# Longer loads for four heads and a shorter load of W2's last rows in a two-layer decode kernel

## The chip, the cores and the metric

The kernel runs on one core of one Trainium2 chip. The metric is the device time of one execution in microseconds; the time given for a kernel is the median of several runs, here 1349.29 us over 3 runs (1348.77 to 1350.27).

## The reference

One token of width 640 goes twice through attention and an MLP, with the same weights and the same cache in both layers:

```python
def _A_ref(x, k_cache, v_cache, wq, wo):
    q = (x @ wq) as 32 heads of 128
    scores = q . k_cache * DH ** -0.5      # 32 heads x 8192 keys x 128
    p = softmax(scores)
    return (p . v_cache) @ wo
def _B_ref(x, w1, w2):
    return maximum(x @ w1, 0) @ w2         # 640 -> 1728 -> 640
x = x + _A_ref(layernorm(x), ...)          # layer 0
x = x + _B_ref(layernorm(x), w1, w2)
x = x + _A_ref(layernorm(x), ...)          # layer 1, the same cache again
x = x + _B_ref(layernorm(x), w1, w2)
```

All of it is float32. The cache of one head is 4 MiB of keys and 4 MiB of values, so one pass over the 32 heads reads 256 MiB. The cache is larger than the on-chip memory and has to be read once for each layer, save what stays on the chip between the two.

## The kernel before

**Order of the work.** Layer 0 goes through heads 0 to 31, layer 1 through heads 31 to 0. What layer 0 read last stays on the chip and is what layer 1 needs first: the last piece of head 29's keys, the last three units of head 30 and all of head 31 are kept (KEPT, 3960 places of 32 bytes in each of 128 partitions). Each head is worked in the same steps: `scores` (L499, TensorE, four matmuls for each piece of keys), `row_maxima` and `exponentials` (VectorE and ScalarE), `values` (L554, TensorE, four matmuls for each piece of values), `output`. At the end of a layer stands the MLP, which reads W2 in 12 blocks that pass through the same ring as the cache, and two more blocks that stay on the chip in `w2_t`.

**The ring and its loads.** Keys, values and W2's twelve blocks go through one tile, `ring`, of RING = 4760 places in each partition. `UNITS` (L42 to 64) says into which units and pieces a head is cut. The list `todo` is the order of all loads; it is written out ahead (L149 to 167), and `pump` (L207) takes its first entry whenever there is room: for an entry without a place, `place` (L181) looks for the tightest gap that holds it whole, for the others `is_free` asks whether the slots are free. Room comes from `release` (L239), which is called behind the last matmul that reads a piece. So each load stands in SyncE's queue behind the one ahead of it, and waits there until the pieces that lay in its place were read. All loads of the ring are issued at L221. One load is one DMA: 128 rows, one for each partition, of as many bytes as the load has places times 32.

**Heads 2 to 26** are loaded by `turning` as whole heads, or in two or three parts where the ring ends; a head is one block in DRAM, with 64 KB for each partition, and a part reads a piece of each of these 64 KB. **Heads 27 to 31** are loaded by units (`all_of`, L127): in DRAM each of their units is a block of its own, the rows of its 128 partitions one behind the other. In layer 0 these heads pass through the first 3072 places alone (L189), since the rest is for what is kept and for W2; four units have a place of their own (`apart`, L123). Layer 1's loads of heads 29, 28 and 27 start where W2's blocks and then the kept pieces have been read. Head 30's two units that are not kept are read into `wct` and `mix` (`load_beside`, L227).

**W2's remainder.** The 1728 rows of W2 are 12 blocks of 128 and 192 rows more. These 192 are laid into two blocks: 128 rows, and 64 rows with 64 rows of zeros behind them (L1043 to 1046). Both are loaded with one DMA of 640 KB on ScalarE's queue at head 7 of layer 0 (L799), and `times_rows` uses only the first 64 partitions of the second block (`rows = 2 * half`).

**ScalarE's queue** also carries the loads of Wq and Wo (L269 to 278), W1 and the row of Wo that is mixed with W1 (L797, L802). `due` (L783) issues those that belong to a head when the head is opened.

Of the kernel before, what the change touches and what calls it, by code (L numbers as in the profile page):

```python
# [15 lines left out]
P = 128  # L16
D = 640
H = 32
# [22 lines left out]
FULL = range(2, 27)  # L41
UNITS = {h: [("kv", K_ALL + V_ALL)] if h <= FULL[-1] else WHOLE for h in range(H)}  # L42
UNITS[0] = [("kv", K_ALL + V_ALL[:3] + [(3, 0, 2), (3, 2, 2)])]
PARTS = {(0, 0): [4, 9], (1, 26): [4, 8], (1, 25): [4, 8], (1, 2): [4, 8], (1, 1): [2, 4, 6, 8], (1, 0): [2, 4, 6, 7, 8, 9]}
UNITS[28] = HALVES
# [17 lines left out]
UNITS[31] = HALVES[:2] + LAST  # L63
DROPPED = {29: 9, 30: 2}
KEPT = 3960
W2_PLACES = 800
# [6 lines left out]
SLOT = RUN // 2  # L73
# [21 lines left out]
F_TILES = 3  # L95
H_CUT = 2 * P
F_REST = 2
FB = 4 * F_TILES + F_REST
W2_RUNS = [range(0, 4), range(4, 8), range(8, 10), range(10, 12)]
UNITS["w2"] = [("w", list(run)) for run in W2_RUNS]  # L100
W2_ALL = [("w2", i) for i in range(len(W2_RUNS))]
RING = KEPT + W2_PLACES


@with_exitstack
def decode_kernel(ctx: ExitStack, tc: tile.TileContext, x, kv, wqo, w1, w2, w2_rest, out):
    nc = tc.nc
# [14 lines left out]
    assert sum(size(UNITS[h][i]) for h, i in kept) == KEPT  # L122
    apart = {(29, 9): (3800, KEPT), (30, 0): (4464, 4544), (30, 1): (4544, RING), (30, 2): (3072, 3800)}  # L123
    beside = [(1, u) for u in order[::-1] if u[0] == 30 and u not in kept]
    todo = []

    def all_of(layer, u):  # L127
        todo.append((layer, u, 0, len(UNITS[u[0]][u[1]][1]), None))

# [7 lines left out]
    def turning(layer, heads, slot):  # L137

        for h in heads:
            for a, end in parts_of(layer, h):  # L140
                while a < end:
                    b = min(end, a + SLOTS - slot)
                    todo.append((layer, (h, 0), a, b, SLOT * slot))
                    slot = (slot + b - a) % SLOTS
                    a = b

    def anywhere(layer, h):
        for a, b in parts_of(layer, h):
            todo.append((layer, (h, 0), a, b, None))  # L149

    for h in range(FULL[0]):
        anywhere(0, h)
    turning(0, FULL, 16)
    for h in range(FULL[-1] + 1, H):
        for i in range(len(UNITS[h])):
            all_of(0, (h, i))
    for u in W2_ALL:
        all_of(0, u)
    for h in range(H)[:FULL[-1]:-1]:
        if h != 30:  # L160
            for i in range(len(UNITS[h])):
                if (h, i) not in kept:
                    all_of(1, (h, i))
    anywhere(1, FULL[-1])
# [4 lines left out]
    for u in W2_ALL:  # L169
        all_of(1, u)  # L170
    source = {}
    for us, dram in ((order, kv), (W2_ALL, w2)):
        o = 0
        for u in us:
            n = 8 * P * size(UNITS[u[0]][u[1]])
            source[u] = dram[o : o + n].rearrange("(p m) -> p m", p=P)
            o += n
    live = {}
# [28 lines left out]
    def pump():  # L207
        while todo:
            layer, u, first, last, at = todo[0]
            unit = UNITS[u[0]][u[1]]  # L210
            ns = [wide(kind_of(unit, t), piece) for t, piece in enumerate(unit[1])]
            n = sum(ns[first:last])
            if at is None:
                at = place(layer, u, n)
                if at is None:
                    return
            elif not is_free(at, n):
                return
            todo.pop(0)
            o = 8 * sum(ns[:first])  # L220
            nc.sync.dma_start(ring[:, 8 * at : 8 * (at + n)], source[u][:, o : o + 8 * n])  # L221
            for t in range(first, last):
                live[layer, u, t] = at, ns[t]
                at_of[layer, u, t] = ring, 8 * at
                at += ns[t]

    def load_beside(where, at, n):  # L227
        layer, u = beside.pop()
        kind, pieces = UNITS[u[0]][u[1]]
        assert 8 * size(UNITS[u[0]][u[1]]) == n  # L230
        nc.sync.dma_start(where[:, at : at + n], source[u])
        for t, piece in enumerate(pieces):
            at_of[layer, u, t] = where, at
            at += 8 * wide(kind, piece)
# [464 lines left out]
    def attention_and_mlp(L, xr, s):  # L699
# [83 lines left out]
        def due(h):  # L783
# [14 lines left out]
            if L == 0 and where == 7:  # L798
                nc.scalar.dma_start(w2_t, w2_rest)  # L799
            if where == 8:  # L800
# [250 lines left out]
def _laid_out(A_x, A_k_cache, A_v_cache, A_wq, A_wo, B_w1, B_w2):  # L1051
# [4 lines left out]
    o = 0  # L1056
    for h in range(H):
        for unit in UNITS[h]:
            n = 8 * size(unit)
            block = kv[o : o + P * n].reshape(P, n)  # L1060
            o += P * n
            a = 0
            for t, piece in enumerate(unit[1]):
                if kind_of(unit, t) == "k":
                    r, c, m = piece
                    part = k[h, :, :, r, c : c + m]
                else:
                    b, r, m = piece
                    part = v[h, :, :, r : r + m, b]
                part = part.reshape(P, -1)  # L1070
                block[:, a : a + part.shape[1]] = part
                a += part.shape[1]
# [7 lines left out]
    for g in range(NG):  # L1080
# [7 lines left out]
        "w2": w2,  # L1088
        "w2_rest": rows[:, 4 * F_TILES :],
    }  # L1090
# [24 lines left out]
```

## Time and profile before

| what | value |
|---|---|
| median of 3 runs | 1349.29 us |
| the profiled execution, its own time | 1349.0 us |
| its span from the first instruction to the last | 1347.2 us |
| TensorE busy | 797.8 us (59%) |
| VectorE busy | 248.3 us (18%) |
| ScalarE busy | 58.5 us (4%) |
| moved by DMA | 574.52 MB, 426 GB/s over the span |

How to read the rows: times are microseconds from the start of the span unless a column says ns. PE is TensorE, DVE VectorE, ACT ScalarE, SP SyncE; a "q" behind a name means its sequencer, where DMAs are issued and waits are spent. L221 is line 221 of the kernel. A row of DMA issues gives the size of one load and the median time from its issue until it has landed. DMA share is the mean busy share of the 16 DMA engines.

### The profile page before, as it was taken

The numbers are of one execution on the slowest core, as the hardware profiler recorded it, in microseconds if no ns is written. First come the engines' busy times: TensorE is split into PE (matmuls) and PEld (weight loads), VectorE is DVE, ScalarE is ACT, GpSimd is POOL, SyncE is SP. The second block draws the span as 40 slices with busy tenths as digits, with TensorE's granted clock in tenths as the row PEclk, the third lists the DMA queues.
The fourth block names the chain that finished last, engine by engine and source line by source line (L and its number), as shares of the span: only waits on it lengthen the run. The fifth ranks groups of instructions, "written<-read, shape, count | busy, mean of one in ns | idle before, by whom it ended". The sixth has DMA issues, their size and how long they took to land.

```text
span 1347.2 us, 13344 instructions
## 1 busy us (share of the span) xinstructions
PE 797.8 (59%) x5966; PEld 261.2 (19%) x5966; DVE 248.3 (18%) x774; ACT 58.5 (4%) x149; POOL 2.9 (0%) x10
## 2 busy tenths in 40 slices
PE   3564445563655664667688754455466654656667
PEld 1121111111211211112252211112121111211214
DVE  1121111121212121112122211122111121111212
ACT  0000000000000000000000000000000000000000
POOL 0000000000000000000000000000000000000000
PEclk9688777778977886788798777898778788878889
DMA  9999999999999999999999999999999999999997
GB/s 413 429 427 437 430 439 428 438 420 428 442 434 422 441 427 423 446 419 419 425 385 425 435 432 436 424 441 429 437 430 430 424 437 436 434 419 438 424 426 326
DMA packets 22673, 574.52 MB, mean 426 GB/s; under 512 B 2516, under 2 KB 2648, under 8 KB 5464
## 3 DMA queue, kind: packets, MB, share of 16 engines
q1 hardware_dynamic: 19592, 529.84, 91.6%
q10 hardware_dynamic: 3024, 43.83, 7.7%
q8 instruction: 47, 0.77, 0.2%
q14 instruction: 10, 0.08, 0.0%
HBM read 573.65 MB, written 0.00 MB: 426 GB/s over the span
## 4 chain that ended last, share of the span: by engine, by line
DMA 65%; PE 26%; DVE 5%; ACT 1%; issue 1%; another core or an unknown queue 1%; ACTq 0%; SPq 0%; DVEq 0%
DMA ring<-in_kv 65%; PE ps L499 13%; PE outs L554 7%; DVE h_t L510 2%; ACT p L524 1%; DVE pt L528 1%; PE pm L515 1%; PE acc L468 1%; PE px L424 1%; DVE p L591 1%; PE px L456 0%; PE px L675 0%; DMA ring<-in_w 0%; DVE pT L530 0%
## 5 line engine op out<-in xcount | busy, mean ns | idle before, releaser
L499 PE MATMUL ps<-ring,spread_q 128*32 128x512 f32 (+3 forms) x2104 | 324.3, 765 | 312.2 <-DMA ring<-in_kv 307.3
L554 PE MATMUL outs<-ring,pT 128*4 128x512 f32 (+1 forms) x2032 | 258.9, 648 | 48.4 <-DVE pT L530 24.4
L499 PEld LDWEIGHTS ps<-ring,spread_q 128*32 128x32 f32 x2104 | 78.2, 137 | 493.2 <-issue 338.5
L510 DVE TENSOR_REDUCE h_t<-ps 128x1 f32<-128x512 f32 x64 | 44.3, 692 | 611.1 <-PE ps L499 611.1
L524 ACT ACTIVATE p<-ps,h_t 128x512 f32<-128x512 f32 x64 | 44.0, 687 | 1223.2 <-DVE h_t L522 1223.2
L554 PEld LDWEIGHTS outs<-ring,pT 128*4 128x4 f32 x2032 | 51.3, 91 | 211.0 <-issue 172.8
L601 PE MATMUL pm<-ones,p 128*128 128x1 f32 x120 | 22.9, 260 | 95.0 <-DVE p L591 95.0
L587 DVE TENSOR_SCALAR p<-outs,ind 128x128 f32<-128x128 f32 x60 | 21.1, 351 | 269.0 <-PE outs L554 269.0
L591 DVE SCALAR_TENSOR_TENSOR p<-outs,ind,p 128x128 f32<-128x128 f32 x180 | 63.1, 351 | 6.4
L528 DVE STREAM_TRANSPOSE pt<-p 128x512 f32<-128x512 f32 x64 | 46.5, 727 | 58.4 <-ACT p L524 58.4
L515 PE MATMUL pm<-row_of,h_t 128*128 128x16 f32 x128 | 26.3, 281 | 49.6 <-DVE h_t L510 48.9
L601 PEld LDWEIGHTS pm<-ones,p 128*128 128x128 f32 x120 | 17.8, 188 | 151.5 <-DVE p L591 150.2
L515 PEld LDWEIGHTS pm<-row_of,h_t 128*128 128x128 f32 x128 | 20.0, 196 | 109.8 <-DVE h_t L510 108.0
L675 PE MATMUL px<-w_t,wct 128*128 128x448 f32 (+1 forms) x80 | 36.7, 574 | 1.0 <-ACT wct L668 1.0
L424 PE MATMUL px<-pair,ln_xc 128*32 128x256 f32 x280 | 34.6, 396 | 4.4 <-ACT mix L683 4.4
L468 PE MATMUL acc<-pair,o_cols 128*32 128x320 f32 x224 | 36.2, 469 | 0.0
L424 PEld LDWEIGHTS px<-pair,ln_xc 128*32 128x32 f32 x280 | 15.7, 113 | 21.4 <-ACT mix L683 8.5
L522 DVE TENSOR_REDUCE h_t<-pm 128x1 f32<-128x16 f32 x64 | 11.2, 175 | 33.0 <-PE pm L515 33.0
L468 PEld LDWEIGHTS acc<-pair,o_cols 128*32 128x32 f32 x224 | 12.9, 117 | 16.8 <-issue 15.7
L675 PEld LDWEIGHTS px<-w_t,wct 128*128 128x128 f32 x80 | 13.8, 197 | 10.8 <-issue 9.3
L530 DVE COPY pT<-pt 128x64 f32<-128x64 f32 x64 | 14.4, 224 | 2.2
L605 DVE COPY o_cols<-pm 128x1 f32<-128x1 f32 x56 | 8.9, 159 | 28.4 <-PE pm L601 28.4
(130 smaller groups left out, 212.1 us busy)
## 6 DMA issues: line engine op xcount, KB each, us to landing
ring<-in_kv SPq DMA_DIRECT2D x24, 4096.0 KB, 31.1
ring<-in_kv SPq DMA_DIRECT2D x11, 6144.0 KB, 36.1
ring<-in_kv SPq DMA_DIRECT2D x31, 2048.0 KB, 35.1
pair<-in_wqo ACTq DMA_DIRECT2D x13, 2560.0 KB, 25.8
ring<-in_kv SPq DMA_DIRECT2D x14, 1024.0 KB, 15.1
ring<-in_w SPq DMA_DIRECT2D x4, 1280.0 KB, 25.9
w_t<-in_w ACTq DMA_DIRECT2D x1, 4320.0 KB, 27.5
pair<-in_wqo ACTq DMA_DIRECT2D x3, 1280.0 KB, 13.1
```

The source lines that it names most:

```text
L424: nc.tensor.matmul(pq[32 * j : 32 * j + 32, :n], xc[:, c : c + 1].to_broadcast([P, 32]), wq_t[g][:, c, j * n : (j + 1) * n], start=(c == 0 ...
L468: nc.tensor.matmul(acc[32 * half : 32 * half + 32, : 2 * DR], col.to_broadcast([P, 32]), wt[:, 2 * half * DR : 2 * (half + 1) * DR], start ...
L499: nc.tensor.matmul(hd.ps[32 * g : 32 * g + 32, c : c + n], spread_q[:, 3 - r : 35 - r], tile_of[:, at + g * n : at + (g + 1) * n], start=f ...
L510: nc.vector.tensor_reduce(hd.nm, hd.ps, AX.X, ALU.max, negate=True)
L515: nc.tensor.matmul(pt[:, :16], hd.nm.to_broadcast([P, P]), row_of.rearrange("p g r -> p (g r)"), start=True, stop=True,)
L524: nc.scalar.activation(hd.p, hd.ps, AF.Exp, bias=hd.low, scale=1.0, accum_out=hd.l)
L528: nc.vector.transpose(pt, hd.p)
L554: nc.tensor.matmul(hd.out[32 * g : 32 * g + 4, r : r + m].rearrange("p r d -> p (r d)"), hd.pT[:, 4 * i : 4 * i + 4], tile_of[:, v : v + m ...
L587: nc.vector.tensor_scalar(oc[:, 0], hd.out[:, 0], ind[:, :1], 0.0, op0=ALU.mult, op1=ALU.add)
L591: nc.vector.scalar_tensor_tensor(oc[:, r], hd.out[:, r], ind[:, r : r + 1], oc[:, r - 1], op0=ALU.mult, op1=ALU.add,)
L601: nc.tensor.matmul(pt[:, :1], oc[:, 3], ones, start=True, stop=True)
L675: nc.tensor.matmul(pt[:, :n], wct[:, c], w1_t[:, c, f : f + n], start=(c == 0), stop=(c == NB - 1),)
```

## The change

**Loads.** `todo` entries now hold a list of pieces that may come from several units, so one load can carry several units that lie one behind the other in DRAM. For that, the rows of DRAM are made longer: all units of a head (for heads 29 and 30: all units of both, in the order that `ROWS` gives) stand in one row for each partition. A row is 64 KB for heads 0 to 28 and 31, and 128 KB for the joint block of 29 and 30. The order of heads stays; within head 29 the last of its keys that are not kept (unit 6) move ahead of its values.

| loads (KB each) | before | after |
|---|---|---|
| layer 0, head 27 | 4096, 4096 | 8192 |
| layer 0, head 28 | 2048 x4 | 4096, 4096 |
| layer 0, head 29 | 1024, 1024, 512, 640, 1024, 1024, 256, 1024, 1024, 640 | 3456, 640, 4096 |
| layer 0, head 30 | 320, 864, 2912, 2048, 2048 | 1184, 2912, 2048, 2048 |
| layer 0, head 31 | 2048, 2048, 2048, 1024, 512, 512 | the same |
| layer 1, head 29 | 1024, 1024, 512, 640, 1024, 1024, 256, 1024, 1024 | 1024, 1024, 512, 640, 3328, 1024 |
| layer 1, head 28 | 2048 x4 | 4096, 2048, 2048 |
| layer 1, head 27 | 4096, 4096 | the same |
| layer 1, head 1 | 2048 x4 | 4096, 4096 |

That is 11 loads fewer in layer 0 and 6 fewer in layer 1.

**W2's remainder.** The 640 KB load becomes one of 320 KB (the 128 rows), and the 64 rows come in eight loads of eight rows of 2560 bytes, one at each of heads 16 to 23 of layer 0, on ScalarE's queue. The eight rows of one load go to partitions that lie four apart: 0, 4, ... 28, then 1, 5, ... 29, and so on to 35, 39, ... 63. The rows of zeros are neither stored nor loaded.

```diff
--- before.py
+++ after.py
@@ -41,7 +41,7 @@
 FULL = range(2, 27)
 UNITS = {h: [("kv", K_ALL + V_ALL)] if h <= FULL[-1] else WHOLE for h in range(H)}
 UNITS[0] = [("kv", K_ALL + V_ALL[:3] + [(3, 0, 2), (3, 2, 2)])]
-PARTS = {(0, 0): [4, 9], (1, 26): [4, 8], (1, 25): [4, 8], (1, 2): [4, 8], (1, 1): [2, 4, 6, 8], (1, 0): [2, 4, 6, 7, 8, 9]}
+PARTS = {(0, 0): [4, 9], (1, 26): [4, 8], (1, 25): [4, 8], (1, 2): [4, 8], (1, 1): [4, 8], (1, 0): [2, 4, 6, 7, 8, 9]}
 UNITS[28] = HALVES
 UNITS[29] = [
     ("k", K_ALL[:1]),
@@ -62,6 +62,34 @@
 ] + HALVES[2:]
 UNITS[31] = HALVES[:2] + LAST
 DROPPED = {29: 9, 30: 2}
+ROWS = [[(h, i) for i in range(len(UNITS[h]))] for h in range(29)]
+ROWS.append([(29, i) for i in (0, 1, 2, 3, 6, 4, 5, 7, 8)] + [(30, 2), (29, 9), (30, 0), (30, 1), (30, 3), (30, 4)])
+ROWS.append([(31, i) for i in range(len(UNITS[31]))])
+ENDS = [
+    [(27, 0), (27, 1)],
+    [(28, 0), (28, 1)],
+    [(28, 2), (28, 3)],
+    ROWS[29][:5],
+    [(29, 9)],
+    ROWS[29][5:9],
+    [(30, 0), (30, 1)],
+    [(30, 2)],
+    [(30, 3)],
+    [(30, 4)],
+] + [[u] for u in ROWS[30]]
+STARTS = [
+    [(29, 0)],
+    [(29, 1)],
+    [(29, 2)],
+    [(29, 3)],
+    ROWS[29][4:8],
+    [(29, 8)],
+    [(28, 0), (28, 1)],
+    [(28, 2)],
+    [(28, 3)],
+    [(27, 0)],
+    [(27, 1)],
+]
 KEPT = 3960
 W2_PLACES = 800
 WIDE = 64
@@ -96,6 +124,7 @@
 H_CUT = 2 * P
 F_REST = 2
 FB = 4 * F_TILES + F_REST
+LAST_AT = [32 * half + i for half in range(2) for i in range(4)]
 W2_RUNS = [range(0, 4), range(4, 8), range(8, 10), range(10, 12)]
 UNITS["w2"] = [("w", list(run)) for run in W2_RUNS]
 W2_ALL = [("w2", i) for i in range(len(W2_RUNS))]
@@ -103,7 +132,7 @@
 
 
 @with_exitstack
-def decode_kernel(ctx: ExitStack, tc: tile.TileContext, x, kv, wqo, w1, w2, w2_rest, out):
+def decode_kernel(ctx: ExitStack, tc: tile.TileContext, x, kv, wqo, w1, w2, w2_rest, w2_last, out):
     nc = tc.nc
     consts = ctx.enter_context(tc.tile_pool(name="consts", bufs=1))
     work = ctx.enter_context(tc.tile_pool(name="work", bufs=1))
@@ -120,12 +149,12 @@
     order = [(h, i) for h in range(H) for i in range(len(UNITS[h]))]
     kept = [u for u in order if u[0] >= min(DROPPED) and u[1] >= DROPPED.get(u[0], 0)]
     assert sum(size(UNITS[h][i]) for h, i in kept) == KEPT
-    apart = {(29, 9): (3800, KEPT), (30, 0): (4464, 4544), (30, 1): (4544, RING), (30, 2): (3072, 3800)}
+    apart = {(29, 9): (3800, KEPT), (30, 0): (4464, RING), (30, 2): (3072, 3800)}
     beside = [(1, u) for u in order[::-1] if u[0] == 30 and u not in kept]
     todo = []
 
-    def all_of(layer, u):
-        todo.append((layer, u, 0, len(UNITS[u[0]][u[1]][1]), None))
+    def all_of(layer, us):
+        todo.append((layer, [(u, t) for u in us for t in range(len(UNITS[u[0]][u[1]][1]))], None))
 
     def parts_of(layer, h):
 
@@ -140,41 +169,43 @@
             for a, end in parts_of(layer, h):
                 while a < end:
                     b = min(end, a + SLOTS - slot)
-                    todo.append((layer, (h, 0), a, b, SLOT * slot))
+                    todo.append((layer, [((h, 0), t) for t in range(a, b)], SLOT * slot))
                     slot = (slot + b - a) % SLOTS
                     a = b
 
     def anywhere(layer, h):
         for a, b in parts_of(layer, h):
-            todo.append((layer, (h, 0), a, b, None))
+            todo.append((layer, [((h, 0), t) for t in range(a, b)], None))
 
     for h in range(FULL[0]):
         anywhere(0, h)
     turning(0, FULL, 16)
-    for h in range(FULL[-1] + 1, H):
-        for i in range(len(UNITS[h])):
-            all_of(0, (h, i))
-    for u in W2_ALL:
-        all_of(0, u)
-    for h in range(H)[:FULL[-1]:-1]:
-        if h != 30:
-            for i in range(len(UNITS[h])):
-                if (h, i) not in kept:
-                    all_of(1, (h, i))
+    for us in ENDS + [[u] for u in W2_ALL]:
+        all_of(0, us)
+    for us in STARTS:
+        all_of(1, us)
     anywhere(1, FULL[-1])
     turning(1, FULL[-2:-1], 0)
     turning(1, FULL[:-2][::-1], 8)
     for h in range(FULL[0])[::-1]:
         anywhere(1, h)
     for u in W2_ALL:
-        all_of(1, u)
+        all_of(1, [u])
     source = {}
-    for us, dram in ((order, kv), (W2_ALL, w2)):
-        o = 0
-        for u in us:
-            n = 8 * P * size(UNITS[u[0]][u[1]])
-            source[u] = dram[o : o + n].rearrange("(p m) -> p m", p=P)
-            o += n
+    o = 0
+    for row in ROWS:
+        n = 8 * sum(size(UNITS[h][i]) for h, i in row)
+        block = kv[o : o + P * n].rearrange("(p m) -> p m", p=P)
+        o += P * n
+        a = 0
+        for h, i in row:
+            source[h, i] = block, a
+            a += 8 * size(UNITS[h][i])
+    o = 0
+    for u in W2_ALL:
+        n = 8 * P * size(UNITS[u[0]][u[1]])
+        source[u] = w2[o : o + n].rearrange("(p m) -> p m", p=P), 0
+        o += n
     live = {}
     at_of = {}
 
@@ -206,29 +237,35 @@
 
     def pump():
         while todo:
-            layer, u, first, last, at = todo[0]
-            unit = UNITS[u[0]][u[1]]
-            ns = [wide(kind_of(unit, t), piece) for t, piece in enumerate(unit[1])]
-            n = sum(ns[first:last])
+            layer, pieces, at = todo[0]
+            ns = []
+            for u, t in pieces:
+                unit = UNITS[u[0]][u[1]]
+                ns.append(wide(kind_of(unit, t), unit[1][t]))
+            n = sum(ns)
             if at is None:
-                at = place(layer, u, n)
+                at = place(layer, pieces[0][0], n)
                 if at is None:
                     return
             elif not is_free(at, n):
                 return
             todo.pop(0)
-            o = 8 * sum(ns[:first])
-            nc.sync.dma_start(ring[:, 8 * at : 8 * (at + n)], source[u][:, o : o + 8 * n])
-            for t in range(first, last):
-                live[layer, u, t] = at, ns[t]
+            u, t = pieces[0]
+            block, o = source[u]
+            unit = UNITS[u[0]][u[1]]
+            o += 8 * sum(wide(kind_of(unit, i), unit[1][i]) for i in range(t))
+            nc.sync.dma_start(ring[:, 8 * at : 8 * (at + n)], block[:, o : o + 8 * n])
+            for (u, t), m in zip(pieces, ns):
+                live[layer, u, t] = at, m
                 at_of[layer, u, t] = ring, 8 * at
-                at += ns[t]
+                at += m
 
     def load_beside(where, at, n):
         layer, u = beside.pop()
         kind, pieces = UNITS[u[0]][u[1]]
         assert 8 * size(UNITS[u[0]][u[1]]) == n
-        nc.sync.dma_start(where[:, at : at + n], source[u])
+        block, o = source[u]
+        nc.sync.dma_start(where[:, at : at + n], block[:, o : o + n])
         for t, piece in enumerate(pieces):
             at_of[layer, u, t] = where, at
             at += 8 * wide(kind, piece)
@@ -796,7 +833,10 @@
             if L == 0 and where == 4:
                 nc.scalar.dma_start(w1_t, w1)
             if L == 0 and where == 7:
-                nc.scalar.dma_start(w2_t, w2_rest)
+                nc.scalar.dma_start(w2_t[:, 0], w2_rest)
+            if L == 0 and 16 <= where < 24:
+                a = LAST_AT[where - 16]
+                nc.scalar.dma_start(w2_t[a : a + 32 : 4, 1], w2_last[where - 16])
             if where == 8:
                 of, nth = divmod(last, HG)
                 nc.scalar.dma_start(
@@ -1054,12 +1094,13 @@
     v = v.transpose(0, 1, 5, 4, 2, 3, 6).reshape(H, P, 4, 4, NBL, DH)
     kv = np.empty(H * P * SK * 2, k.dtype)
     o = 0
-    for h in range(H):
-        for unit in UNITS[h]:
-            n = 8 * size(unit)
-            block = kv[o : o + P * n].reshape(P, n)
-            o += P * n
-            a = 0
+    for row in ROWS:
+        n = 8 * sum(size(UNITS[h][i]) for h, i in row)
+        block = kv[o : o + P * n].reshape(P, n)
+        o += P * n
+        a = 0
+        for h, i in row:
+            unit = UNITS[h][i]
             for t, piece in enumerate(unit[1]):
                 if kind_of(unit, t) == "k":
                     r, c, m = piece
@@ -1086,7 +1127,8 @@
         "wqo": wqo,
         "w1": np.asarray(B_w1).reshape(NB, P, DFF).transpose(1, 0, 2),
         "w2": w2,
-        "w2_rest": rows[:, 4 * F_TILES :],
+        "w2_rest": rows[:, 4 * F_TILES],
+        "w2_last": np.stack([rows[a : a + 32 : 4, 4 * F_TILES + 1] for a in LAST_AT]),
     }
```

## Rows read from the trace of the kernel before

**Rows 1.** The page: its span, and the rate of all DMA in 40 slices.
```profile
span 1347.2 us, 13344 instructions
...
GB/s 413 429 427 437 430 439 428 438 420 428 442 434 422 441 427 423 446 419 419 425 385 425 435 432 436 424 441 429 437 430 430 424 437 436 434 419 438 424 426 326
```

**Rows 2.** The page, the chain that ended last, shares by engine.
```profile
DMA 65%; PE 26%; DVE 5%; ACT 1%; issue 1%; another core or an unknown queue 1%; ACTq 0%; SPq 0%; DVEq 0%
```

**Rows 3.** Stretches: length, busy PE, PEld, DVE, ACT, POOL, PEclk, DMA share, GB/s.
```profile
20.00:560.00 540.00, 297.33 (x1994) 89.05 (x1986) 93.36 (x276) 21.65 (x55) 0.00 (x0) 0.79 1.00 432
600.00:640.00 40.00, 29.36 (x220) 8.65 (x216) 10.13 (x33) 1.56 (x4) 0.00 (x0) 0.89 0.99 418
640.00:690.00 50.00, 33.81 (x364) 14.06 (x360) 9.32 (x29) 3.08 (x8) 0.00 (x0) 0.85 1.01 424
690.00:700.00 10.00, 9.17 (x188) 6.55 (x176) 2.83 (x15) 0.37 (x3) 0.00 (x0) 1.00 0.80 318
700.00:716.00 16.00, 13.33 (x184) 6.56 (x184) 3.86 (x17) 0.78 (x2) 1.10 (x2) 1.00 1.01 406
760.00:1300.00 540.00, 313.91 (x2102) 95.34 (x2102) 97.35 (x290) 22.83 (x58) 0.00 (x0) 0.81 1.00 431
```

**Rows 4.** Waits of SyncE's queue from 588 to 760 us: total, times, longest.
```profile
SPq L221 <- DMA ring<-in_kv: 46.7, 17, 9.4
```

**Rows 5.** Three single loads: time of issue, then size and time to landing.
```profile
569.52 0.33 SPq L221 DMA_DIRECT2D ring<-in_kv  x1
...
ring<-in_kv SPq DMA_DIRECT2D x1, 4096.0 KB, 29.6
...
576.76 0.33 SPq L221 DMA_DIRECT2D ring<-in_kv  x1
...
ring<-in_kv SPq DMA_DIRECT2D x1, 4096.0 KB, 32.1
...
636.49 0.33 SPq L221 DMA_DIRECT2D ring<-in_kv  x1
...
ring<-in_kv SPq DMA_DIRECT2D x1, 640.0 KB, 15.1
```

**Rows 6.** Head 27's scores on TensorE, in order of time: start, length.
```profile
605.10 1.06 PE L499 MATMUL ps<-ring,spread_q 128*32 128x512 f32 x8
...
606.62 2.78 PE L499 MATMUL ps<-ring,spread_q 128*32 128x512 f32 x24
```

**Rows 7.** The second load of head 28's keys: issue, size and time to landing.
```profile
592.01 0.33 SPq L221 DMA_DIRECT2D ring<-in_kv  x1
...
ring<-in_kv SPq DMA_DIRECT2D x1, 2048.0 KB, 26.6
```

**Rows 8.** W2's last load in layer 0: issue, size and time to landing.
```profile
696.55 0.33 SPq L221 DMA_DIRECT2D ring<-in_w  x1
...
ring<-in_w SPq DMA_DIRECT2D x1, 640.0 KB, 4.9
```

**Rows 9.** Head 31's scores in layer 1 (chain); the fourth load of head 29.
```profile
707.43 3.71 PE ps L499 x32
...
702.30 0.33 SPq L221 DMA_DIRECT2D ring<-in_kv  x1
...
ring<-in_kv SPq DMA_DIRECT2D x1, 640.0 KB, 13.6
```

**Rows 10.** W2's remainder on ScalarE's queue; ScalarE's waits from 340 to 520 us.
```profile
166.52 0.34 ACTq L799 DMA_DIRECT2D w_t<-in_w_rest  x1
...
w_t<-in_w_rest ACTq DMA_DIRECT2D x1, 640.0 KB, 24.7
...
ACT p L524 <- DVE h_t L522: 178.7, 9, 30.1
```

**Rows 11.** The page's DMA issues: loads of three quarters of a head.
```profile
ring<-in_kv SPq DMA_DIRECT2D x11, 6144.0 KB, 36.1
```

## The prediction, made before the change was run

> **What bounds the kernel now.** I read the page first. Its rate of DMA stands between 385 and 446 GB/s in all slices but the last, over a span of 1347.2 us [rows 1], and the chain that ended last is DMA for 65% [rows 2]. A chain alone doesn't say whether the transfers or the latency between them are the limit, so I cut the run into stretches next [rows 3]. From 20 to 560 us, where heads of 8192 KB come in one to three loads, the 16 DMA engines are busy with a share of 1.00 and move 432 GB/s; from 760 to 1300 us it is 1.00 and 431. The kernel there is as long as its bytes. Three stretches around the change of layer move less: 418 GB/s (600 to 640 us), 424 (640 to 690) and 406 (700 to 716), all at a share of 0.99 to 1.01, so the engines are not out of work there but do their work in smaller portions. One stretch is short of work: 690 to 700 us, with a share of 0.80 and 318 GB/s, where layer 0's MLP has to be finished before places come free.
>
> Last I looked at SyncE's queue between 588 and 760 us: 17 times, 46.7 us in all, a load there waited for the landing of an earlier load and not for a reader [rows 4]. The change lessens such waits, as it has fewer loads. They are priced at nothing: the DMA engines had a share of 1.00 while they lasted [rows 3], so what they held back would have stood in line anyway.
>
> **The price of one load.** In layer 0 the second half of head 27 lands at 576.76 + 32.1 = 608.86 us, and the last unit of head 29 at 636.49 + 15.1 = 651.59 us [rows 5]. In these 42.73 us come the 14 loads of heads 28 and 29, 16384 KB, and 1280 KB of Wo, together 18.09 MB. At 432 GB/s that is 41.87 us; 0.86 us is left, 0.06 us for each of the 14 loads. The long loads next to them check the rate: head 27's two halves land 608.86 - 599.12 = 9.74 us apart, 4.19 MB at 431 GB/s [rows 5].
>
> Seventeen loads fewer then give 17 x 0.06 = 1.0 us. All of it lies on the path, because the DMA engines are the bound on either side. The bounds: nothing, if the shortfall of these stretches comes from something other than the number of loads; and all of it, if longer loads restore 432 GB/s, which is (14/432) x 40 + (8/432) x 50 + (26/432) x 16 = 1.3 + 0.9 + 1.0 = 3.2 us [rows 3]. I take 1.0, worked out from the loads themselves; the stretch from 700 us keeps its four short first loads, and layer 0's head 31 keeps its six.
>
> **What longer loads hold back.** A longer load waits for a longer gap, and its readers wait for all of it. There are three places.
>
> Head 27 of layer 0 is now one load. It goes where the second half went (576.76 us) and lands at 608.8 us with it, whereas TensorE was ready for its keys at 605.10 us and took until 609.40 [rows 6]. So the keys are read by 608.8 + 4.3 = 613.1 us. Behind that stands the load of head 28's values, for which head 27's keys must have gone. The queue meanwhile holds head 28's keys, which land as before at 592.01 + 26.6 = 618.6 us [rows 7]. How early must a load be issued to follow without a gap? W2's last load met a nearly idle queue and took 4.9 us to land [rows 8]; 1.5 us of that are its 655 KB at 432 GB/s, so 3.4 us are lead. The values have to go by 618.6 - 3.4 = 615.2 us; they go at 613.1, which leaves 2.1 us. Price: nothing; if that cover is gone, each us that TensorE is later costs one.
>
> In layer 1, units 6, 4, 5 and 7 of head 29 become one load that needs both halves of head 31's keys read: 707.43 + 3.71 = 711.1 us [rows 9]. The load ahead of it lands at 702.30 + 13.6 = 715.9 us, less 3.4 of lead is 712.5 us: 1.4 us of cover, price nothing, bound 1.0 us. Behind this load in SyncE's queue stand all others of layer 1; the next ones (unit 8, head 28's keys) need head 30's keys and head 31's values read, which comes later still, so none of them is held up by it. Head 28's keys as one load land with their second half. Head 1's two loads of 4096 KB need gaps of 1024 places in place of 512; head 2's 8192 KB stand in line ahead of them, price nothing.
>
> Head 29's unit 6 now lands ahead of its values, and its values land together. In layer 0 its values are read after their last piece is there, and then head 30's 1184 and 2912 KB stand in line, 9.7 us at 432 GB/s. Nothing is charged.
>
> **W2's remainder.** The zeros are 64 x 2560 bytes = 0.164 MB, 0.38 us at 432 GB/s. That is the gain if all 16 engines share it. The bounds follow from who is relieved: if eight engines had carried the zeros, each has 20,480 bytes less, 0.76 us at 432/16 = 27 GB/s, which counts in full if the slowest engine is among them and not at all if it isn't.
>
> The eight new loads cost between nothing and 8 x 0.06 = 0.48 us; I take half, as each has only eight rows: 0.24 us. Net -0.14 us. ScalarE issues each in 0.34 us [rows 10] just ahead of a head's exponentials. It waited 178.7 us for VectorE in nine waits between 340 and 520 us [rows 10], so the issues are hidden; if not, it is 8 x 0.34 = 2.7 us. They go at heads 16 to 23 of 32, and the one load of 640 KB took 24.7 us beside long loads [rows 10], so TensorE doesn't wait for them in the MLP.
>
> [...]
>
> **The sum.** -1.02 (loads) - 0.38 + 0.24 (W2) + 0 (holding back) = -1.2 us against the profiled execution's 1349.0, that is 1347.8. The median of the runs shown is 0.3 us higher, 1349.29; on that scale the forecast is 1348.1 us. A change within 0.2% (2.7 us) can't be told from none in this kernel, so I forecast no change that shows.
>
> **Rivals.**
> 1. *The short loads were the whole shortfall.* Then 3.2 us come back and W2's relief is the full 0.76: 1349.29 - 4.0 = 1345.3 us. For it: the share is 1.0 at 418 GB/s, so the engines lose time within the transfers [rows 3]. Against it: 0.06 us for a load explains all the excess between 609 and 652 us. Chance 0.16.
> 2. *Slower: the row spacing of 128 KB.* Heads 29 and 30 now lie in DRAM with 128 KB from one partition's row to the next; head 28's and 27's rows are 64 KB apart. The joint block is read for 16384 KB in layer 0, 7552 KB in layer 1 and 1184 KB beside the ring: 25.7 MB, 59.5 us at 432 GB/s. If that spacing cost x%, the time would rise by 0.595 us for each percent: 5% gives 1349.29 - 1.2 + 3.0 = 1351.1 us, and it shows as slower from 6.6% on (3.9 us), 1352.0. Half the rate would be 59.5 us, 1407.6. Against it: the eleven loads of 6144 KB and the other parts of heads already read pieces of rows 64 KB apart [rows 11], in stretches that run at 432 GB/s [rows 3]. No row shows 128 KB. Chance of 6.6% or more: 0.05.
>    [...]
> 3. *The cover at head 27 is gone.* TensorE reads head 27's keys over 6 us later than worked out; the DMA engines then stand idle for 4 us and more and the result is slower, some 1352 us. It would take other work of TensorE between the landing and the scores; rows 6 show 4.3 us for all of it, the side work included. Chance 0.03.
>
> **How the numbers follow.** The forecast has 0.76; its own range runs from -1.02 - 0.76 to 0.48 + 1.0, that is 1347.5 to 1350.8 us. The range given reaches down into rival 1, to 1345.6, and ends at 1350.8 us. Faster by over 0.2% is rival 1: 0.16. Slower by over 0.2% is rivals 2 and 3: 0.08. The rest, 0.76, is no change.
>
> **What would show it.** Right: the stretches 600 to 640 and 640 to 690 us some 3 to 5 GB/s faster, 690 to 700 us as poor as it is, head 27's scores some 4 us later, and the stretch around 613 to 620 us at a share near 1. The rival of the spacing would show as heads 29 and 30 moving at well under 420 GB/s in both layers. Wrong: a drop of the DMA share around 615 or 713 us, ScalarE waiting in its queue at heads 16 to 23, or a gain that lies outside 560 to 760 us, which no step here provides.

## The result, and the profile after

The changed kernel takes 1354.56 us (median of 6 runs, 1353.61 to 1355.95) against 1349.40 us before (6 runs): 5.2 us slower, ratio 1.0037 with a 95% interval of 1.0027 to 1.0047. Forecast were 1348.1 us and no change that shows.

The two profiled executions have spans of 1347.2 and 1353.4 us, 6.2 us apart. The page of the changed kernel, the lines that answer to [rows 1]:

```profile
span 1353.4 us, 13316 instructions
...
GB/s 417 421 432 432 445 418 435 435 425 440 429 428 425 438 431 431 440 423 385 424 377 409 434 430 428 433 439 429 441 434 425 427 437 431 432 425 435 426 427 300
```

One slice stands out whose counterpart before kept up with its neighbours (419 GB/s): the nineteenth, 609 to 643 us, at 385 GB/s. The stretches of the changed kernel (some lie within others), columns as in [rows 3]:

```profile
20.00:560.00 540.00, 298.19 (x1994) 89.13 (x1986) 93.26 (x276) 21.65 (x55) 0.00 (x0) 0.79 1.00 432
600.00:620.00 20.00, 12.04 (x68) 3.55 (x64) 3.69 (x12) 0.78 (x2) 0.00 (x0) 0.74 0.84 348
612.00:614.00 2.00, 2.00 (x16) 0.55 (x12) 0.00 (x0) 0.00 (x0) 0.00 (x0) 0.50 0.68 295
614.00:616.00 2.00, 2.00 (x12) 0.20 (x4) 0.00 (x0) 0.00 (x0) 0.00 (x0) 0.50 0.51 205
612.00:620.00 8.00, 5.41 (x32) 1.45 (x28) 1.96 (x6) 0.78 (x2) 0.00 (x0) 0.71 0.69 260
712.00:718.00 6.00, 5.08 (x32) 1.01 (x24) 0.77 (x2) 0.00 (x0) 0.00 (x0) 0.73 0.83 348
760.00:1300.00 540.00, 325.19 (x2086) 96.98 (x2082) 97.97 (x291) 22.93 (x58) 0.00 (x0) 0.79 1.00 431
```

and two of the same stretches before:

```profile
612.00:620.00 8.00, 5.70 (x50) 1.71 (x51) 2.56 (x10) 0.00 (x0) 0.00 (x0) 1.00 1.00 424
712.00:718.00 6.00, 6.00 (x70) 2.04 (x74) 1.82 (x4) 0.78 (x2) 0.00 (x0) 1.00 1.01 421
```

The long stretches are untouched, 432 and 431 GB/s in both. The DMA engines run short of work in two places where they had none missing: at 612 to 620 us (share 0.69 for 1.00, 8 x 0.31 = 2.5 us of their time) and at 712 to 718 us (0.83 for 1.01, 1.1 us). And the granted clock of TensorE (third column from the end) is lower in both, 0.71 and 0.73 for 1.00.

**At head 27 of layer 0.** TensorE's instructions in order (start, length), then the issue of head 28's values on SyncE:

```profile
604.19 0.38 PE L638 MATMUL pm<-ones,p 128*128 128x1 f32 x2 [1.65 <-DVE p L628]
608.30 1.94 PE L536 MATMUL ps<-ring,spread_q 128*32 128x512 f32 x8 [3.72 <-DMA ring<-in_kv]
610.16 1.01 PE L476 MATMUL px<-sel,q_row 64*128 64x2 f32 x4
611.11 5.31 PE L536 MATMUL ps<-ring,spread_q 128*32 128x512 f32 x24
...
616.49 0.33 SPq L257 DMA_DIRECT2D ring<-in_kv  x1
```

TensorE idles 3.72 us until the whole head has landed, and then the scores last until 616.4 us, 8.1 us from their start; before they took 4.3 [rows 6]. Eight matmuls take 1.94 us where they took 1.06, and 24 take 5.31 where they took 2.78: the granted clock was 0.50 from 608 to 616 us, where it was 1.00 before (605.1 to 609.4 us). Head 28's values, one load behind head 27's keys, go at 616.49 us. The DMA engines run short before that: their share is 0.68 from 612 to 614 us already.

How much is lost here differs from execution to execution. Two of the experiments below, the one with head 1 in quarters and the one with head 29 apart, have the same layer 0. In their profiles TensorE waits 2.95 and 2.99 us, the scores take 7.1 us in both (the eight 1.93 and 1.94 us, the 24 4.28), the values go at 615.05 and 615.17 us, and the share from 612 to 620 us is 0.81 and 0.80. The first of the two:

```profile
612.00:620.00 8.00, 5.61 (x32) 1.58 (x28) 1.97 (x6) 0.78 (x2) 0.00 (x0) 0.71 0.81 330
```

**At the start of layer 1.** Head 31's scores take 5.35 us in place of 3.71 [rows 9], at a granted clock of 0.67 while they ran, for 1.00 before, and the long load of head 29 goes when they are done:

```profile
711.73 5.35 PE L536 MATMUL ps<-ring,spread_q 128*32 128x512 f32 x32 [0.46 <-DVE spread_q L526]
...
717.10 0.33 SPq L257 DMA_DIRECT2D ring<-in_kv  x1
```

**At the end of layer 1.** Head 1's two pairs of values (L591), and the last matmuls of the kernel, after the change:

```profile
1317.94 1.90 PE L591 MATMUL outs<-ring,pT 128*4 128x512 f32 x16 [1.20 <-DMA ring<-in_kv]
1319.77 2.31 PE L427 MATMUL px<-w_t 128*128 128x512 f32 x4
1322.01 1.90 PE L591 MATMUL outs<-ring,pT 128*4 128x512 f32 x16
...
1329.55 1.93 PE L536 MATMUL ps<-ring,spread_q 128*32 128x512 f32 x16
...
1348.83 1.29 PE L493 MATMUL px<-ring,hT 128*32 128x160 f32 x32
```

and before:

```profile
1309.17 1.90 PE L554 MATMUL outs<-ring,pT 128*4 128x512 f32 x16 [0.64 <-DVE pT L530]
1311.00 2.31 PE L390 MATMUL px<-w_t 128*128 128x512 f32 x4
1313.67 1.90 PE L554 MATMUL outs<-ring,pT 128*4 128x512 f32 x16 [0.36 <-DMA ring<-in_kv]
...
1323.46 1.92 PE L499 MATMUL ps<-ring,spread_q 128*32 128x512 f32 x16 [1.29 <-DMA ring<-in_kv]
...
1342.73 1.29 PE L456 MATMUL px<-ring,hT 128*32 128x160 f32 x32
```

Before, only the second half of head 1's values was left to do when it landed at 1313.67 us; the last matmuls start 29.1 us later. After, both halves begin at 1317.94 us, when the one load is there, and it is 30.9 us to the last matmuls. Before, TensorE still waited 1.29 us for the last keys of head 0 (1323.46 us); after, it comes to them at 1329.55 us without a wait, so that its own work, and no longer a landing, leads from there to the end. So 1.8 us of the 6.1 us by which these start later arose after the last values of head 1 had landed. The other 4.3 us were there when head 31's scores began (711.73 against 707.43).

### The profile page after: what moved, and what is told of

Its sections match the earlier page's. It is cut to its first block, busy times and chain, and to the rows that moved or that the text cites. A ratio compares the mean times of both kernels' runs of the same rounds, so it can differ in the third digit from the quotient of the medians.

```text
span 1353.4 us, 13316 instructions
## 1 busy us (share of the span) xinstructions
PE 818.6 (60%) x5966; PEld 266.0 (20%) x5966; DVE 248.0 (18%) x774; ACT 58.6 (4%) x149; POOL 2.9 (0%) x10
## 4 chain that ended last, share of the span: by engine, by line
DMA 62%; PE 29%; DVE 5%; ACT 1%; issue 1%; another core or an unknown queue 1%; ACTq 0%; SPq 0%; DVEq 0%
DMA ring<-in_kv 62%; PE ps L536 14%; PE outs L591 9%; DVE h_t L547 2%; ACT p L561 1%; DVE pt L565 1%; PE acc L505 1%; PE pm L552 1%; DVE p L628 1%; PE px L461 1%; PE px L493 0%; DMA ring<-in_w 0%; PE px L712 0%; DVE pT L567 0%
## 5 line engine op out<-in xcount | busy, mean ns | idle before, releaser
L536 PE MATMUL ps<-ring,spread_q 128*32 128x512 f32 (+3 forms) x2104 | 332.6, 783 | 298.2 <-DMA ring<-in_kv 293.3
L591 PE MATMUL outs<-ring,pT 128*4 128x512 f32 (+1 forms) x2032 | 267.7, 664 | 47.1 <-DMA ring<-in_kv 24.1
L591 PEld LDWEIGHTS outs<-ring,pT 128*4 128x4 f32 x2032 | 52.4, 93 | 216.5 <-issue 171.8
L461 PE MATMUL px<-pair,ln_xc 128*32 128x256 f32 x280 | 37.4, 420 | 4.2 <-ACT mix L720 4.2
```

The lines of the kernel that those rows point to most:

```text
L461: nc.tensor.matmul(pq[32 * j : 32 * j + 32, :n], xc[:, c : c + 1].to_broadcast([P, 32]), wq_t[g][:, c, j * n : (j + 1) * n], start=(c == 0 ...
L536: nc.tensor.matmul(hd.ps[32 * g : 32 * g + 32, c : c + n], spread_q[:, 3 - r : 35 - r], tile_of[:, at + g * n : at + (g + 1) * n], start=f ...
L591: nc.tensor.matmul(hd.out[32 * g : 32 * g + 4, r : r + m].rearrange("p r d -> p (r d)"), hd.pT[:, 4 * i : 4 * i + 4], tile_of[:, v : v + m ...
```

## The experiments

Each was timed in 5 rounds against the kernel before, on the same chip as the others of its group. "Theory A" is that longer loads are read too late, "B" that the rows in DRAM 128 KB apart cost bandwidth, "C" that W2's eight loads cost. What an undone part is worth is the difference of its ratio from the changed kernel's 1.0037, which was not measured beside it; with intervals of some 0.001 to either side, two ratios less than about 0.0014 apart can't be told from each other. The lines under a run are from one of its executions, and that need not be a middle one: with head 29 apart it was the slowest of the run, with all three apart the fastest.

### Head 1 again in quarters

```diff
-(1, 1): [4, 8],
+(1, 1): [2, 4, 6, 8],
```

> The change, but head 1 of layer 1 again in four loads of 2048 KB. Theory A (longer loads are read too late): head 0 is the last head and its work starts behind head 1's; in the changed kernel head 1's values are there only at the end of their 4096 KB, so the last chain on TensorE is about 1.9 us later than the last landing would need (the last load of W2 landed some 4.2 us later than before, the end came 6.1 us later). Undone: 1.5 to 2.5 us faster than the changed kernel, about 1.0022 to 1.0029 of the kernel before. Theory B (rows 128 KB apart in DRAM cost bandwidth): head 1 is not in those rows, so no more than 0.5 us. Theory C (the eight loads of W2's rows cost): no more than 0.5 us.

Measured: 1351.71 us against 1349.77, ratio 1.0014 [1.0005, 1.0023], so 0.0023 or 3.1 us less than the changed kernel. As A forecast, if with more than the 1.5 to 2.5 us it had, and against B and C: head 1 lies neither in the rows 128 KB apart nor near W2.

### Head 27 again in halves

```diff
-    [(27, 0), (27, 1)],
+    [(27, 0)],
+    [(27, 1)],
```

> The change, but head 27 of layer 0 again as two loads of 4096 KB (keys, then values). Theory A: TensorE no longer waits 3.7 us for the whole head, its clock is not granted at half when head 27's scores run, head 28's values are issued some 4 to 8 us earlier (about 609 in place of 616.5 us), the DMA share from 612 to 620 us is back near 1.0, and the kernel is 1.5 to 3.5 us faster than the changed one. Theory B: the DMA share there stays low in spite of the earlier issue, and the time moves by less than 0.5 us. Theory C: less than 0.5 us.

Measured: 1352.88 us, 1.0020 [1.0011, 1.0030], 0.0017 or 2.3 us less than the changed kernel. Its stretch, the longer part of head 27's scores and the issue of head 28's values:

```profile
612.00:620.00 8.00, 5.79 (x38) 1.47 (x42) 2.07 (x9) 0.00 (x0) 0.00 (x0) 0.79 1.00 428
...
606.41 2.78 PE L537 MATMUL ps<-ring,spread_q 128*32 128x512 f32 x24
...
609.25 0.33 SPq L258 DMA_DIRECT2D ring<-in_kv  x1
```

As A forecast: the issue is 7.2 us earlier, the share is 1.00 again, and the rate of 428 GB/s lies above the 424 of before: heads 28 and 29 still come in longer loads.

### Head 29's four units apart in layer 1

```diff
-    ROWS[29][4:8],
+    [(29, 4)],
+    [(29, 5)],
+    [(29, 6)],
+    [(29, 7)],
```

> The change, but units 4, 5, 6 and 7 of head 29 in layer 1 again as four loads. Theory A: the first of them is issued some 2.5 to 4 us earlier than the one long load (717.1 us in the changed kernel), the drop of the DMA share from 716 to 718 us is gone, and the kernel is 1 to 2 us faster than the changed one. Theory B (row spacing): the four loads move well under 420 GB/s wherever they are issued, and the time stays or gets worse. Theory C: less than 0.5 us.

Measured: 1354.12 us, 1.0030 [1.0019, 1.0042]. That is 0.0007 less than the changed kernel, which the intervals don't tell from nothing: inconclusive in the time. Its stretches and head 31's scores:

```profile
712.00:718.00 6.00, 5.54 (x36) 2.06 (x32) 0.69 (x3) 0.00 (x0) 0.00 (x0) 0.50 1.01 419
716.00:722.00 6.00, 5.07 (x36) 0.97 (x28) 0.77 (x2) 0.00 (x0) 0.00 (x0) 0.69 0.95 359
...
714.11 6.39 PE L539 MATMUL ps<-ring,spread_q 128*32 128x512 f32 x32 [0.46 <-DVE spread_q L529]
```

Here the scores start 2.4 us later than in the changed kernel and take 6.39 us, at a granted clock of 0.50 from 712 to 718 us. The share is 1.01 up to 718 us, and around the end of the scores, from 716 to 722 us, it is 0.95 at 359 GB/s: with the four loads apart a gap is left, if a smaller one. The run with the rows in DRAM alone (below) has the four loads apart as well, slow scores (5.18 us) and a gap:

```profile
712.00:718.00 6.00, 5.07 (x42) 1.37 (x38) 0.88 (x3) 0.00 (x0) 0.00 (x0) 0.86 0.91 325
```

The run with head 1 in quarters keeps the long load, and head 31's scores took 3.64 us, at a granted clock of 1.00 from 712 to 718 us:

```profile
710.98 3.64 PE L536 MATMUL ps<-ring,spread_q 128*32 128x512 f32 x32 [0.46 <-DVE spread_q L526]
...
714.64 3.50 SPq L257 DMA_DIRECT2D ring<-in_kv  x2
...
712.00:718.00 6.00, 5.08 (x50) 1.39 (x42) 1.03 (x4) 0.78 (x2) 0.00 (x0) 1.00 1.01 395
```

Its share is 1.01, though the rate is down to 395 GB/s. So the gap is there with four loads too and is not the long load's alone; in these executions it comes with slow scores, but a low clock doesn't always bring it (from 710 to 720 us the run with the rows in DRAM alone has a granted clock of 0.82 and a share of 0.96, the one with head 27 in one load and the other two apart 0.81 and 1.01). What sets the clock of an execution here was not settled.

### All three apart

The three edits above together. Of the 17 loads of the ring 11 are still saved, ten of them in layer 0 (not 10 in all, as the expectation has it); the long rows and W2's part stay.

> All three undone at once: head 27 in halves, head 29's four units apart in layer 1, head 1 in quarters. What stays of the change: the long rows in DRAM, the longer loads of heads 28, 29 and 30 in layer 0 and of head 28's keys in layer 1 (10 loads fewer), W2's eight loads. Theory A: the whole loss is gone, within 1.5 us of the kernel before, more likely 0.5 us faster than slower. Theory B and theory C: still 4 to 5 us slower than the kernel before (1.003 to 1.004).

Measured: 1350.16 us, 1.0001 [0.9992, 1.0010]. The whole loss is gone; B and C, which would have kept 4 to 5 us, fall. Whether anything is gained can't be told from the time. The rates show what the longer loads do where they hold nothing back:

```profile
600.00:640.00 40.00, 29.57 (x198) 8.13 (x186) 9.69 (x32) 1.56 (x4) 0.00 (x0) 0.83 1.01 431
640.00:690.00 50.00, 38.98 (x400) 16.06 (x400) 9.53 (x31) 3.08 (x8) 0.00 (x0) 0.90 1.00 421
```

431 GB/s from 600 to 640 us where it was 418 [rows 3]. Other runs bear it out: 430 and 429 GB/s with head 27 in halves and in the last run below, which have longer loads there too, and 416 to 421 in the three with the loads of before. From 640 us on, where head 31's loads and W2's are as short as before, nothing is gained.

### W2's rows alone

```diff
-nc.scalar.dma_start(w2_t, w2_rest)
+nc.scalar.dma_start(w2_t[:, 0], w2_rest)
...
+    nc.scalar.dma_start(w2_t[a : a + 32 : 4, 1], w2_last[where - 16])
```

> The kernel before with the change to W2's last 64 rows alone (the 128 rows in one load of 320 KB, the 64 rows in eight loads of eight rows). Theory A gives W2's part nothing that shows: within 1 us of the kernel before (head 26 landed 0.2 us later in the changed kernel, when all eight loads were in). Theory C (the eight loads are what costs): 2 us slower or more.

Measured: 1349.04 us against 1349.69, 0.9996 [0.9987, 1.0005]. Not slower, so C falls on its own too; a gain of 0.4 us and none are both inside.

### The rows in DRAM alone

`ROWS` as in the change, `ENDS` and `STARTS` with one unit for each load, W2 and head 1 as before.

> The kernel before with the new rows in DRAM alone: every load as before, but heads 27, 28 and 31 read from rows 64 KB apart and heads 29 and 30 from rows 128 KB apart. Theory A: within 1 us of the kernel before, and the rates from 600 to 690 us as before (418 and 424 GB/s). Theory B (the spacing costs bandwidth): 2 us slower or more, with lower rates where heads 29 and 30 are moved.

Measured: 1349.85 us, 1.0001 [0.9992, 1.0010].

```profile
600.00:640.00 40.00, 28.20 (x236) 8.41 (x232) 10.37 (x33) 1.56 (x4) 0.00 (x0) 0.96 1.00 419
640.00:690.00 50.00, 32.35 (x344) 13.26 (x340) 9.32 (x29) 2.99 (x8) 0.00 (x0) 0.83 1.01 424
```

419 and 424 GB/s where it was 418 and 424: rows 128 KB apart cost nothing that shows. B falls.

### Head 27 in one load alone

The kernel above, with head 27's units in one load.

> The new rows in DRAM and head 27 of layer 0 as one load of 8192 KB, all other loads as in the kernel before. Head 28's values still come as two loads, so the first of them can go when half of head 27's keys are read. Theory A: TensorE waits some 3.7 us before head 27's scores, these run at half the clock, and the DMA share from 610 to 620 us falls below 0.95, but somewhat less than in the changed kernel: 1 to 3 us slower than the kernel before. If the loss at head 27 needs head 28's values in one load too, it is within 1 us.

Measured: 1351.27 us, ratio 1.0005 [0.9997, 1.0014]: smaller than expected and not told from no change.

```profile
600.00:620.00 20.00, 11.13 (x65) 3.45 (x60) 3.69 (x12) 0.78 (x2) 0.00 (x0) 0.72 0.92 383
```

The wait (4.63 us) and the slow scores (1.94 us for the eight, 4.77 for the 24; granted clock 0.72 from 600 to 620 us) are there, but with head 28's values in two loads the share is 0.92, against 0.84 to 0.89 in the three executions with one.

### Head 1 in halves alone

The first experiment's edit the other way round, on the kernel before.

> The kernel before with nothing changed but head 1 of layer 1 in two loads of 4096 KB. Theory A: the last landing comes as before and the end 1.5 to 2.5 us later, as TensorE's last chain starts from the later landing of head 1's values: 1.0011 to 1.0018. Theories B and C: no change.

Measured: 1351.69 us, 1.0017 [1.0008, 1.0026], 2.3 us. Its values of head 1 and last matmuls:

```profile
1314.01 1.90 PE L554 MATMUL outs<-ring,pT 128*4 128x512 f32 x16 [1.21 <-DMA ring<-in_kv]
...
1344.89 1.29 PE L456 MATMUL px<-ring,hT 128*32 128x160 f32 x32
```

The same 30.9 us from one to the other as in the changed kernel, with everything else of the change away.

### TensorE kept busy ahead of head 27

```diff
 hd = opened(where)
+if not L and h == 27:
+    keep_busy(3, bank="pm")
```

> The change with three matmuls of 512 columns of W1 more, whose result nobody reads, on TensorE ahead of head 27's scores in layer 0, where TensorE otherwise waits 3.7 us for head 27. Theory A1 (the wait lowers the granted clock, and the slow scores are what lets the DMA engines run dry): head 27's scores take about 4.3 us in place of 8.1, head 28's values are issued at some 612.7 us in place of 616.5, the DMA share from 612 to 620 us is above 0.9 and the kernel is 1.5 to 3 us faster than the changed one. Theory A2 (the later landing alone is what costs, the clock is by the way): the scores still end at 615 us or later, or the DMA share stays low, and the time moves by less than 0.7 us.

Measured: 1352.47 us, 1.0018 [1.0010, 1.0027], 0.0019 or 2.6 us less than the changed kernel, with one more piece of work in it.

```profile
604.78 5.08 PE L427 MATMUL pm<-w_t 128*128 128x512 f32 x6 [0.25 <-DVE o_cols L642]
609.78 1.07 PE L536 MATMUL ps<-ring,spread_q 128*32 128x512 f32 x8
610.78 0.60 PE L476 MATMUL px<-sel,q_row 64*128 64x2 f32 x4
611.31 2.78 PE L536 MATMUL ps<-ring,spread_q 128*32 128x512 f32 x24
...
614.15 0.33 SPq L257 DMA_DIRECT2D ring<-in_kv  x1
...
612.00:620.00 8.00, 5.61 (x40) 1.61 (x36) 1.97 (x6) 0.78 (x2) 0.00 (x0) 0.77 0.91 372
```

The added matmuls took 5.08 us, where four of the same shape take 2.31 us at a granted clock of 1.00 (1319.77 us above), and so put off the scores by 1.5 us; but these then take 4.3 us as before, the values go 2.3 us earlier than in the changed kernel, and the share rises to 0.91, from 0.69 there and 0.80 and 0.81 in the other two executions of that layer 0. Of the DMA engines' time 0.7 us (8 x 0.09) is still missing. So the slow scores are the larger part of the loss there, but not all of it.

### Head 28's values in halves

```diff
-    [(28, 2), (28, 3)],
+    [(28, 2)],
+    [(28, 3)],
```

> The change with head 28's values in layer 0 as two loads of 2048 KB in place of one of 4096 KB. Theory A: the first of them can go when half of head 27's keys are read, some 3 to 4 us ahead of the end of the scores (about 612.5 us), so the DMA engines have less of a gap: share from 600 to 620 us about 0.92 in place of 0.84, and 0.7 to 2 us faster than the changed kernel. If the order of issue doesn't matter: no change.

Measured: 1353.14 us, 1.0022 [1.0009, 1.0034], 0.0015 or 2.0 us less.

```profile
600.00:620.00 20.00, 12.05 (x72) 3.56 (x64) 3.69 (x12) 0.78 (x2) 0.00 (x0) 0.74 0.93 392
...
613.15 0.33 SPq L258 DMA_DIRECT2D ring<-in_kv  x1
```

Wait and clock are those of the changed kernel (3.72 us, and 0.74 from 600 to 620 us in both); the first half goes at 613.15 us and the share is 0.93, as expected. The time alone doesn't decide it, as its interval overlaps the changed kernel's 1.0027 to 1.0047. By the shares the gap at head 27 takes three things: one load for the head, one load behind its keys, and the slow scores between.

### Head 27 in one load, the other two apart

Head 1's and head 29's edits of above, head 27 in one load.

> As the run with three parts undone, but with head 27 of layer 0 in one load again: head 29's units and head 1 stay apart. Theory A: the loss at head 27 by itself in this kernel, 1.5 to 3 us slower than with head 27 in halves (1.0012 to 1.0023 of the kernel before), the last landing of head 31 in layer 0 near 692.4 us and not 690. If head 1 and head 29's units were the whole loss: as the kernel before.

Measured: 1351.70 us, 1.0013 [1.0005, 1.0022]: 0.0012 or 1.6 us more than with all three apart, at the low end of what was expected and at the edge of what can be told. This kernel differs from the one with head 1 in quarters only in head 29's four loads, and that one measured 1.0014: nothing to be seen of the long load of head 29.

### What seems worth keeping

W2's part, and longer loads for heads 29 and 30 of layer 0 only.

> What seems worth keeping: W2's eight loads and the longer loads of heads 29 and 30 in layer 0 (8 loads fewer); heads 27 and 28, layer 1's head 29 and head 1 as in the kernel before. Theory A: nothing is read later than before, 8 x 0.06 = 0.5 us from the loads and about 0.4 us from W2's part: 0.5 to 1.5 us faster than the kernel before, 0.9989 to 0.9996, at the edge of what can be told from no change.

Measured: 1349.08 us against 1349.65, 0.9995 [0.9986, 1.0003]. The medians have the expected sign and size; from no change it can't be told. No version was found that beats the kernel before beyond doubt.

## Why the prediction was wrong

**The step that failed** is "What longer loads hold back", in two of its places.

At head 27 two terms failed, the length of the scores and the limit for the next load. It let the scores take 4.3 us, their length before, from [rows 6], behind a wait of 3.7 us that it had worked out itself. Landing (608.8 against some 608.2 us) and wait (3.7) came as worked out; the scores took 8.1 us, the values went at 616.5 us and not 613.1, and the limit it had set, 615.2 us, was missed (in the two other executions of this layer 0 the scores took 7.1 us). The duration was taken from a row that TensorE had reached without a long wait: it began as the matmuls ahead of it ended, which had waited 1.65 us, and the granted clock was 1.00 from 605.1 to 609.4 us:

```profile
604.78 0.38 PE L601 MATMUL pm<-ones,p 128*128 128x1 f32 x2 [1.65 <-DVE p L591]
```

The limit was wrong as well. Its lead of 3.4 us came from one load that met a nearly idle queue [rows 8]. But the share is down to 0.68 from 612 us on, and the executions in which the values went in time by that limit, at 615.05, 615.17 and (with TensorE kept busy) 614.15 us, lost 1.5, 1.6 and 0.7 us of the DMA engines' time all the same. Through these three and the changed kernel's 2.5 us at 616.49 us the loss would begin near 613.2 us (an estimate): the cover of 2.1 us was not there, and every microsecond by which the values went later cost some 0.8 us of the engines' time. What came is the forecast's third rival, given 0.03, with the wrong cause: no other work of TensorE's that had been left out stood between landing and scores, and the 4 us of idle it priced were 2.5. The sign of being wrong that the forecast had named, a drop of the share around 615 or 713 us, is what the profile shows.

At head 1 it asked only whether the DMA queue runs dry. It doesn't: the share lies between 0.96 and 1.02 from 1305 to 1340 us. But head 1 is the last head but one, and TensorE's chain behind its values sets the end: 1.8 us in the profile, 2.3 us with this edit alone. The price of nothing was wrong, and the work behind the landing was not looked at.

For head 29 in layer 1 the price of nothing, with a bound of 1.0 us, is not refuted: 1.1 us of the DMA engines' time were missing there in the changed kernel, but with the four loads apart the time was 0.0007 less, which is not told from nothing, and a gap was seen with four loads too.

**What was right.** The spacing of rows costs nothing that shows (1.0001), and W2's part stays within its bounds (0.9996); which engines carried the zeros, on which the 0.76 us of its range rests, no run shows. From 600 to 640 us, with all three parts apart, 431 GB/s against 418 is 40 x 13/431 = 1.2 us, twice what ten loads at 0.06 us make and close to the upper bound of 1.3. So the gain of a microsecond is there in the rates of that stretch. In the time it is not shown, with all three parts apart either (1.0001), and in the changed kernel it was more than spent: about 2.3 us at head 27 and 2.3 to 3.1 at head 1 by the undone parts; the rest is not assigned to a place. ScalarE's issues of W2's rows took about twice the 0.34 us assumed (last section), which cost nothing that shows.

**What stays open.** Of the 4.3 us by which layer 1's first scores start later in the changed kernel's profile, 2.75 were there at head 31's last values (694.38 against 691.63 us). The wait for W2's last block is 0.6 us longer (0.96 against 0.37 us), and 1.0 us comes from 708 us on, where the granted clock was 0.59 up to 710.2 us, for 1.00 before (704.7 to 706.1 us). After and before:

```profile
708.06 2.09 PE L438 MATMUL px<-pair,ln_xc 128*32 128x128 f32 x40
...
704.74 1.30 PE L401 MATMUL px<-pair,ln_xc 128*32 128x128 f32 x40
```

Three executions of one and the same layer 0 differ in the clock ahead of this (0.77, 1.00 and 0.72 from 680 to 690 us), so part of the delay may come from the clock that an execution was granted there; it was not tried by itself. The executions with parts of the change also scatter more than those of the kernel before, with head 27 in halves from 1350.33 to 1355.87 us against 1348.89 to 1352.50 beside it, and no run shows why.

## What to carry to other kernels

Where one engine's work frees the places of the next loads, a longer load can cost twice, as at head 27: its reader starts later, and here it ran slower as well, 24 matmuls in 4.28 to 5.35 us behind waits of 2.95 to 4.63 us, where they took 2.78 before. (With head 1 in halves alone they took 5.35 us without such a wait, so it is not shown that the wait is what slows them.) So a cover has to be worked out with the slow durations, and its limit not from a single load on an idle queue. Behind the last loads of a kernel it is not the transfers but the work left when they land that counts (here 30.9 us of it for 29.1): there a load should be cut so that little is left to do behind the last piece. Merging loads was worth 0.06 us each by the forecast's estimate and 0.12 by the rates (1.2 us for ten), so that one microsecond of delay undoes eight merges or more.

## What the runs showed of the hardware

The issue of a load of eight rows holds ScalarE's queue longer than that of a load of 128 rows, 0.63 to 0.66 us against 0.34 [rows 10], and the first of the eight 1.21 us. One of them:

```profile
404.30 0.63 ACTq L839 DMA_DIRECT2D w_t<-in_w_last  x1
```

No run here shows why these issues are longer, or why the first took twice as long as the others.
